# An attention and feed-forward block on one core: last pairs of a slot issued ahead of the block's copy, key differences ahead of the parts, reciprocal deviations in steps

## The chip, the cores and the metric

The kernel runs on one core of a Trainium2 chip. The metric is the device time of one execution in microseconds; the median over several executions is given. The core's engines work from queues of their own and meet only at semaphores: TensorE (PE in the profile, with its weight loads as PEld), VectorE (DVE), ScalarE (ACT), GpSimd (POOL), and SyncE (SP), which here issues most transfers.

## The reference

One transformer block in float32: layer normalisation, attention of 32 heads with 20 columns each over 2048 tokens of width 640, the input added; then a second normalisation, a gated feed-forward part of width 1728, and the sum again.

```python
def _A_ref(x, wqkv, wo):          # B, S, D = 1, 2048, 640; H = 32; Dh = 20
    qkv = (x @ wqkv).reshape(B, S, 3, H, Dh).transpose(2, 0, 3, 1, 4)
    q, k, v = qkv[0], qkv[1], qkv[2]
    scores = jnp.einsum("bhqd,bhkd->bhqk", q, k) * (Dh ** -0.5)
    p = _softmax(scores, axis=-1)
    o = jnp.einsum("bhqk,bhkd->bhqd", p, v)
    return o.transpose(0, 2, 1, 3).reshape(B, S, D) @ wo
def _B_ref(x, w_gate, w_up, w_down):
    return (_silu(x @ w_gate) * (x @ w_up)) @ w_down
h = x + _A_ref(_layernorm(x), A_wqkv, A_wo)
h2 = h + _B_ref(_layernorm(h), B_w_gate, B_w_up, B_w_down)
```

## The kernel before

The program has three stages: the projections to queries, keys and values; attention; and the output projection with the feed-forward part. The order of the work is written out by hand, and each engine runs its instructions in the order in which the program issues them. To get float32 precision out of faster matmuls, an operand is kept in two parts, `hi` and `lo`; `split` (L84) makes them, `hi` as a copy on ACT (L85), `lo` as a difference on DVE or POOL (L86).

**Projections.** The tokens come in four chunks `c` of 512. Chunk `c` has ten blocks of 128 columns (even `m` are keys, odd `m` queries; `query_key`, L429, fifteen matmuls) and eight value pieces (`value`, L500, fifteen matmuls of 320 columns). Each is a slot, numbered 18·c + j. Chunk 0 runs its blocks first, then its values; chunks 1 and 2 run five key blocks (j 0 to 4), five query blocks (j 5 to 9), eight values; chunk 3 runs keys, values, queries. In the last slots of a chunk, at j = 12 to 16 in chunk 0 and 11 to 15 in chunks 1 and 2, `flip` (L405) transposes the next chunk's normalised input: TensorE into a `ps_one` buffer, then on ACT a copy (L281) and `hi` (L85), `lo` on POOL.

The results of a block go through `keep` (L462): from slot 8 on ACT copies the block out of its buffer (L481); the parts are made in the next slot, when `finish_keep` or the next `keep` calls what was put off; then the stores are issued on ACT's own queue (L426), each block's in the slot after it. Before slot 8 the parts are made straight from the buffer, and for keys the difference of the block's two halves after them (copy L475 on ACT, subtraction L476 on DVE). A value is copied from its buffer by ACT (L517, the ev copy).

**Maxima in the projections.** The softmax needs the maximum of each query's scores over 512 keys. A part of these maxima, 288 pairs of head pairs, is computed between the projections' matmuls. `max_pair` (L170) takes two matmuls and a DVE reduction over 512 columns (L180). `max_halves` (L184) uses max(a, b) = b + relu(a − b) with the key differences: two matmuls (L188), a relu on ACT (L193), and two fused operations on DVE (L195). The operands of `max_halves` are loaded back from where the blocks were stored, as items in four `raw` tiles (`load_items`, `stack`, on SP, L148); `ready` says when an item may be used: two slots after its load was issued. Two lists hold the pairs, `urgent` (unit 0 with `max_pair`) and `early` (`max_halves`), and `visit(n)` (L358) issues up to n pairs from them that are ready. A `query_key` of chunks 1 to 3 visits once in its middle, after nine matmuls (three pairs), and the main loop visits after every slot, three pairs after a block and two after a value; a value visits in its middle too (two pairs).

**Buffers.** PSUM holds three `ps_wide` tiles of two banks (pairs; blocks of the first slots) and two `ps_one` tiles of one bank (later blocks, values, transpositions), each kind used in turn: the next user of a buffer waits until the last reader is done.

**Attention.** 32 units (a group of four heads by a chunk of queries) of sixteen steps. A step's order is in `ORDER`: scores (L950) with their exponentials on ACT (L956), the remaining maxima one at a time (matmul L204, DVE L210), and `weigh` (L960), eight matmuls with the values. In the last units `projection` runs beside it, one entry of the list `extra` a step: the output projection (L688), the sums and statistics on DVE, the reciprocal standard deviations (`moments`, fourteen small DVE operations of L95 by a first guess and three refinements, `rstd_steps`, L88), the application to the first token tile, and transpositions (L716).

Of the kernel before, what the change touches and what calls it, by code (L numbers as in the profile page):

```python
# [44 lines left out]
def tile_block(ctx: ExitStack, tc: tile.TileContext, x, wqkv, wo, wg, wu, wd, out):  # L45
# [30 lines left out]
    def ps_one():  # L76
        return psum.tile([P, CH], F32, name="ps_one", tag="ps_one", bufs=2)
# [190 lines left out]
    with tc.tile_pool(name="pa", bufs=2) as pa:  # L268
# [43 lines left out]
        def staged_keys(g, c, kc, k, q):  # L312
            def one(t, pair):
                max_halves(mxs[g * NC + c], items[q][3], items[k][3], pair, t, kc)
                for n in (k, q):
                    users[n] -= 1
                load_items()

            def ready():
                return all(items[n][3] is not None and slot[0] >= items[n][4] + 2 for n in (k, q))  # L320

            pairs = [(t, pair) for t in moved(g * NC + c, kc) for pair in range(2)]
            for n in (k, q):
                users[n] += len(pairs)
            return [(ready, lambda a=a: one(*a)) for a in pairs]
# [24 lines left out]

        urgent = [a for kc in range(NC) for a in in_unit(0, kc, 18 * kc + 7)]
        early = [a for g in range(1, NG) for a in staged(g, (0, 0))]
        early += staged(1, (0, 1)) + staged(2, (0, 1))
        early += [a for g in range(3) for a in staged(g, (1, 1), (1, 0))]
# [74 lines left out]
        def query_key(c, m):  # L429

            z_hi, z_lo = zs[c]
            ps = ps_wide()[:, 0, :] if slot[0] < 7 else ps_one()
            for n, (a, w) in enumerate(((z_hi, w_hi), (z_lo, w_hi), (z_hi, w_lo))):
                for k in range(ND):
                    nc.tensor.matmul(  # L435
                        ps, w[:, k, m * P : (m + 1) * P], a[:, k, :],
                        start=(n == 0 and k == 0), stop=(n == 2 and k == ND - 1),
                    )
                    if n == 1 and k == 3 and c:
                        visit(3)  # L440
            keep(c, m, ps)
# [22 lines left out]
        def keep(c, m, ps):  # L464
# [7 lines left out]
            if slot[0] < 8:  # L472
                split(ps, hi[:, :CH], lo[:, :CH], nc.vector)
                if which:
                    nc.scalar.activation(over, ps[:, half:], AF.Copy)  # L475
                    nc.vector.tensor_tensor(  # L476
                        out=over, in0=ps[:, :half], in1=over, op=ALU.subtract
                    )
                    halved.append(lambda: split(over, hi[:, CH:], lo[:, CH:], nc.gpsimd))
            else:  # L480
# [20 lines left out]
        def value(c, t, half):  # L501
# [5 lines left out]
            for a, w in ((z_hi, w_hi), (z_hi, w_lo), (z_lo, w_hi)):  # L507
                for k in range(ND):
# [5 lines left out]
                    if n == 9 and slot[0] > 9:  # L514
                        visit(2)
            dst = ev[:, half * 4 : half * 4 + 4, : G * VW].rearrange("p g (h w) -> p g h w", h=G)
            nc.scalar.activation(  # L517
# [39 lines left out]
        for c in range(NC):  # L557
# [7 lines left out]
            for j, (kind, *which) in enumerate(work):  # L565
# [11 lines left out]
                if which:  # L577
# [4 lines left out]
                    else:  # L582
                        (query_key if kind == "block" else value)(c, *which)
                visit(2 if kind == "value" else 3)
                finish_keep()
# [70 lines left out]
    def projection(c, ps_of):  # L656
# [41 lines left out]

        def moments():
            rs.append(rstd_of(pc, mv[:, :, 1], TPC, "c"))  # L700

# [25 lines left out]
        def first(t, half):  # L727
# [8 lines left out]
            [lambda t=t, half=half: first(t, half) for t in range(TPC) for half in range(2)],  # L736
            [moments, lambda: apply(0)],
            [lambda t=t: flip(t) for t in range(TPC)],
# [287 lines left out]
    for u in range(NU):  # L1026
        g, c = divmod(u, NC)
        if g == NG - 1 and c >= 2:
            _, first, ln, flips, _ = ahead
            extra = [*first, ln[0], lambda: None, ln[1], lambda: None, *flips]  # L1030
        for kt in range(NT):
# [626 lines left out]
```

## Time and profile before

| | us |
|---|---|
| median of three executions | 2107.35 (2106.49 to 2111.93) |
| the profiled execution's own time | 2110.45 |
| its span, first to last instruction | 2108.7 |
| projections | 0 to 389.5 |
| attention | 389.5 to 1536.5 |
| output projection and feed-forward | 1536.5 to 2108.7 |

The mean granted clock of TensorE over the span is 0.995 of full speed. The page's slices show its busy share and its clock, in tenths, in 40 slices of 52.7 us:

```
PE   7999999999999999999999999999999999999998
PEclk9999999999999999999999999999999999999999
```

The projections are the first seven or so of these slices. A timeline row has the start and the duration of a group of equal instructions, the engine, the line, the output and input tiles by name, and in brackets the idle time before it with the instruction that ended it. A window's row has the busy times of the engines inside two borders.

### The profile page before, as it was taken

The numbers are of one execution on the slowest core, as the hardware profiler recorded it, in microseconds if no ns is written. First come the engines' busy times: TensorE is split into PE (matmuls) and PEld (weight loads), VectorE is DVE, ScalarE is ACT, GpSimd is POOL, SyncE is SP. The second block draws the span as 40 slices with busy tenths as digits, with TensorE's granted clock in tenths as the row PEclk, the third lists the DMA queues.
The fourth block names the chain that finished last, engine by engine and source line by source line (L and its number), as shares of the span: only waits on it lengthen the run. The fifth ranks groups of instructions, "written<-read, shape, count | busy, mean of one in ns | idle before, by whom it ended". The sixth has DMA issues, their size and how long they took to land.

```text
span 2108.7 us, 37142 instructions
## 1 busy us (share of the span) xinstructions
PE 2066.6 (98%) x12636; PEld 1207.3 (57%) x12636; DVE 1659.5 (79%) x3631; ACT 1445.4 (69%) x2835; POOL 691.2 (33%) x949
## 2 busy tenths in 40 slices
PE   7999999999999999999999999999999999999998
PEld 5656566433333433334333433335578888888888
DVE  6767867788888888888888988886368766666677
ACT  3647575899999999999999999996743222212221
POOL 2231110233443424353420001001135434653555
PEclk9999999999999999999999999999999999999999
DMA  8565544335263443543631213131137755884642
GB/s 257 174 205 179 164 140 127 87 116 153 88 183 103 148 140 118 156 139 133 188 111 56 52 32 94 34 115 61 35 121 266 263 169 188 298 301 159 196 152 94
DMA packets 197285, 305.38 MB, mean 145 GB/s; under 512 B 47440, under 2 KB 82256, under 8 KB 196072
## 3 DMA queue, kind: packets, MB, share of 16 engines
q1 hardware_dynamic: 183512, 274.15, 41.2%
q10 hardware_dynamic: 13584, 28.85, 4.6%
q8 instruction: 102, 1.67, 0.4%
q14 instruction: 87, 0.71, 0.1%
HBM read 203.82 MB, written 98.30 MB: 143 GB/s over the span
## 4 chain that ended last, share of the span: by engine, by line
PE 87%; DVE 6%; DMA 3%; issue 2%; ACT 1%; ACTq 1%; POOL 0%; SPq 0%; DVEq 0%; POOLq 0%
PE acc L960 24%; PE ps_one L950 15%; PE ps_a L1121 15%; PE ps_max L204 12%; PE ps_b L1215 8%; PE ps_one L509 3%; PE ps_wide L188 3%; PE ps_one L435 3%; DVE over L195 2%; PE ps_max L688 2%; DVE mx L180 2%; PE ps_b L688 1%; DMA halves<-j_d 1%; ACTq L426 1%; ACT over L193 0%
## 5 line engine op out<-in xcount | busy, mean ns | idle before, releaser
L956 ACT ACTIVATE probs<-ps_one 128x512 f32<-128x512 f32 x2048 | 1056.9, 616 | 66.1 <-PE ps_one L950 41.3
L210 DVE TENSOR_REDUCE mx<-ps_max 128x1 f32<-128x512 f32 x1472 | 925.6, 683 | 109.3 <-PE ps_one L950 77.6
L950 PE MATMUL ps_one<-q_stk,k_stk 62*128 62x512 f32 x2048 | 586.4, 451 | 2.6 <-DVE m L86 1.7
L960 PE MATMUL acc<-probs,v_stk 128*32 128x512 f32 x4096 | 547.2, 607 | 0.0
L950 PEld LDWEIGHTS ps_one<-q_stk,k_stk 62*128 62x128 f32 x2048 | 251.6, 184 | 432.9 <-ACT probs L956 397.1
L204 PE MATMUL ps_max<-k_stk,q_stk 60*128 60x512 f32 x1472 | 381.7, 425 | 1.4 <-DVE mx L210 1.3
L204 PEld LDWEIGHTS ps_max<-k_stk,q_stk 60*128 60x128 f32 x1472 | 271.9, 186 | 26.6 <-DVE mx L210 2.7
L195 DVE CUSTOM_DVE_ANT_0 over<-ps_wide,over 128x256 f32<-128x256 f32 x512 | 184.7, 420 | 82.9 <-ACT over L193 82.8
L1336 DVE TENSOR_TENSOR tmp<-ps_a,tmp 128x512 f32<-128x512 f32 x208 | 141.2, 689 | 119.9 <-PE ps_a L1121 94.1
L193 ACT ACTIVATE over<-ps_wide 128x512 f32<-128x512 f32 x256 | 138.6, 597 | 76.9 <-PE ps_wide L188 32.2
L1215 PE MATMUL ps_b<-halves,yp 128*128 128x320 f32 x1032 | 179.3, 308 | 2.0 <-DMA halves<-j_d 1.2
L960 PEld LDWEIGHTS acc<-probs,v_stk 128*32 128x32 f32 x4096 | 80.7, 108 | 175.3 <-issue 166.7
L1215 PEld LDWEIGHTS ps_b<-halves,yp 128*128 128x128 f32 x1032 | 165.1, 188 | 18.6 <-POOL yp L86 1.5
L995 POOL TENSOR_TENSOR o<-o,rb 128x512 f32<-128x512 f32 x31 | 39.9, 1286 | 411.2 <-DMA q_stk<-q_d 178.8
L1121 PE MATMUL ps_a<-t,units 128*128 128x512 f32 x624 | 162.6, 396 | 0.0
L1121 PE MATMUL ps_a<-z,units 128*128 128x512 f32 x516 | 133.9, 394 | 0.0
L1121 PEld LDWEIGHTS ps_a<-t,units 128*128 128x128 f32 x624 | 112.6, 188 | 18.8 <-ACT tmp L1349 0.2
L86 POOL TENSOR_TENSOR yp<-y,yp 128x256 fp32r<-128x256 f32 x96 | 60.2, 627 | 188.3 <-ACT yp L85 188.3
L188 PE MATMUL ps_wide<-raw 60*128 60x512 f32 x512 | 107.6, 468 | 12.3 <-DVE mx L195 7.1
L1220 DVE TENSOR_TENSOR h<-ps_b,h 128x320 f32<-128x320 f32 x248 | 109.9, 480 | 6.9 <-PE ps_b L1215 5.4
L1121 PEld LDWEIGHTS ps_a<-z,units 128*128 128x128 f32 x516 | 93.1, 187 | 15.9
L85 ACT ACTIVATE yp<-tmp 128x512 fp32r<-128x512 f32 x40 | 25.3, 632 | 103.1 <-POOL tmp L1208 103.1
(189 smaller groups left out, 2195.5 us busy)
## 6 DMA issues: line engine op xcount, KB each, us to landing
units<-w_d SPq DMA_DIRECT2D x186, 256.0 KB
w_d<-stage SPq DMA_DIRECT2D x106, 256.0 KB
halves<-j_d SPq DMA_DIRECT2D x70, 320.0 KB
j_d<-stage SPq DMA_DIRECT2D x42, 320.0 KB
k_stk<-k_d SPq DMA_DIRECT2D x64, 160.0 KB
q_stk<-q_d SPq DMA_DIRECT2D x64, 160.0 KB
raw<-k_d SPq DMA_DIRECT2D x54, 160.0 KB
rb<-r_d SPq DMA_DIRECT2D x32, 256.0 KB
```

What stands on the lines that cost most here:

```text
L188: nc.tensor.matmul(ps[:, b, :], q[rows, pair, t * P : (t + 1) * P], k[rows, pair, :], start=True, stop=True,)
L193: nc.scalar.activation(over, ps[:, :, CH // 2 :], AF.Relu)
L195: nc.vector.tensor_tensor_reduce(over[:, b], ps[:, b, : CH // 2], over[:, b], 1.0, LOWEST, ALU.add, ALU.max, mx[:, b, pair, t, kc : kc + 1],)
L204: nc.tensor.matmul(ps, queries[u][rows, pair, t * P : (t + 1) * P], keys[u // NC][rows, pair, kc * CH : (kc + 1) * CH], start=True, stop=True,
L210: nc.vector.tensor_reduce(mxs[u][:, b, pair, t, kc : kc + 1], ps, axis=AX.X, op=ALU.max)
L950: nc.tensor.matmul(ps, keys[u // NC][rows, p, kt * P : (kt + 1) * P], queries[u][rows, p, :], start=True, stop=True,)
L956: nc.scalar.activation(probs[p][:, b, :], ps, AF.Exp, scale=scale)
L960: nc.tensor.matmul(acc[32 * j : 32 * j + 32, :], values[u // NC][:, kt, j * VW : j * VW + 32], probs[j // 2][:, j % 2, :], start=(kt == 0) ...
L1121: nc.tensor.matmul(ps.rearrange("p (t n) -> p t n", t=TPC), w[k][:, i], z[k][:, :, j], start=(first and m == 0), stop=(last and m == len(n ...
L1215: nc.tensor.matmul(ps, a, b, start=(n == 0), stop=(n == len(pairs) - 1))
L1220: nc.vector.tensor_tensor(out=h, in0=ps, in1=h, op=ALU.add)
L1336: add = lambda out, ps, x: nc.vector.tensor_tensor(out=out, in0=ps, in1=x, op=ALU.add)
```

## The change

It has five edits in the projections and one in attention.

1. `ready`: in slots below 24 an item may be used three slots after its load was issued, later two as before.
2. The eight pairs of unit 0 against the second chunk of keys leave `urgent` (where they were `max_pair`) and join `early` as `max_halves`; two more items are loaded for them.
3. The block of slot 6 uses a `ps_one` buffer; before, it used half a `ps_wide`.
4. Pairs ahead of the copies: in chunks 1 to 3 a block's last `visit(3)` is issued before `keep`, so before its copy; in the middle it visits two pairs where m is a multiple of four, three otherwise. A value's last `visit(2)` is issued before the ev copy. The main loop's own visit is left for the blocks of chunk 0.
5. In the slots below 8 the key difference (L475, L476) is issued ahead of the parts (L85, L86).
6. `moments` runs in three attention steps, five, five and four of its operations, and the application follows in the third. Before, all fourteen ran in one step, and the application two steps later. The list `extra` keeps its length.

```diff
             def ready():
-                return all(items[n][3] is not None and slot[0] >= items[n][4] + 2 for n in (k, q))
+                return all(items[n][3] is not None and slot[0] >= items[n][4] + 2 + (slot[0] < 24) for n in (k, q))
...
-        urgent = [a for kc in range(NC) for a in in_unit(0, kc, 18 * kc + 7)]
+        urgent = [a for kc in (0, 2, 3) for a in in_unit(0, kc, 18 * kc + 7)]
         early = [a for g in range(1, NG) for a in staged(g, (0, 0))]
-        early += staged(1, (0, 1)) + staged(2, (0, 1))
+        early += [a for g in range(3) for a in staged(g, (0, 1))]
...
-            ps = ps_wide()[:, 0, :] if slot[0] < 7 else ps_one()
+            ps = ps_wide()[:, 0, :] if slot[0] < 6 else ps_one()
...
                     if n == 1 and k == 3 and c:
-                        visit(3)
+                        visit(2 if m % 4 == 0 else 3)
+            if c:
+                visit(3)
             keep(c, m, ps)
...
             if slot[0] < 8:
-                split(ps, hi[:, :CH], lo[:, :CH], nc.vector)
                 if which:
                     nc.scalar.activation(over, ps[:, half:], AF.Copy)
                     nc.vector.tensor_tensor(
                         out=over, in0=ps[:, :half], in1=over, op=ALU.subtract
                     )
+                split(ps, hi[:, :CH], lo[:, :CH], nc.vector)
+                if which:
                     halved.append(lambda: split(over, hi[:, CH:], lo[:, CH:], nc.gpsimd))
...
                     if n == 9 and slot[0] > 9:
                         visit(2)
+            visit(2)
             dst = ev[:, half * 4 : half * 4 + 4, : G * VW].rearrange("p g (h w) -> p g h w", h=G)
...
-                visit(2 if kind == "value" else 3)
+                if c == 0 and kind != "value":
+                    visit(3)
                 finish_keep()
...
-        def moments():
-            rs.append(rstd_of(pc, mv[:, :, 1], TPC, "c"))
+        chain = []
+
+        def moments(i):
+            if not rs:
+                r, steps = rstd_steps(pc, mv[:, :, 1], TPC, "c")
+                rs.append(r)
+                chain.extend(steps)
+            for f in chain[5 * i : 5 * i + 5]:
+                f()
...
-            [moments, lambda: apply(0)],
+            [lambda: moments(0), lambda: moments(1), lambda: (moments(2), apply(0))],
...
-            extra = [*first, ln[0], lambda: None, ln[1], lambda: None, *flips]
+            extra = [*first, *ln, lambda: None, *flips]
```

## The prediction

> **What bounds the kernel now.** I read the head of the page, the table of windows, then the timeline at the places that the diff touches. First the span, the engines' busy times and the engines' shares of the chain that ended last.
>
> ```profile
> span 2108.7 us, 37142 instructions
> PE 2066.6 (98%) x12636; PEld 1207.3 (57%) x12636; DVE 1659.5 (79%) x3631; ACT 1445.4 (69%) x2835; POOL 691.2 (33%) x949
> PE 87%; DVE 6%; DMA 3%; issue 2%; ACT 1%; ACTq 1%; POOL 0%; SPq 0%; DVEq 0%; POOLq 0%
> ```
>
> TensorE is busy for 98%, and the diff takes no matmul away: the maxima of all 288 pairs stay, so only TensorE's idle and slowly clocked time can shrink. Next the windows: borders and length, busy time and instructions of PE, PEld, DVE, ACT, POOL, then granted clock, DMA share, GB/s. The first two are projections and attention; the third holds the blocks of chunk 1, the fourth its slot 21; the last three lie in the attention step that the diff's last part touches.
>
> ```profile
> 0.00:389.51 389.51, 361.29 (x1773) 247.42 (x1773) 281.22 (x1210) 228.02 (x420) 79.29 (x66) 0.98 0.58 175
> 389.51:1536.50 1146.99, 1143.64 (x7890) 469.86 (x7890) 976.97 (x1653) 1080.66 (x2132) 314.40 (x472) 1.00 0.35 105
> 97.71:163.85 66.14, 60.15 (x257) 39.49 (x256) 45.68 (x184) 33.03 (x59) 19.32 (x15) 0.95 0.71 205
> 114.86:126.93 12.07, 8.64 (x28) 5.26 (x26) 4.14 (x21) 3.62 (x7) 3.27 (x3) 0.72 0.73 220
> 1464.00:1468.00 4.00, 2.71 (x17) 0.90 (x15) 3.55 (x18) 3.37 (x7) 0.00 (x0) 1.00 0.35 139
> 1468.00:1472.00 4.00, 3.88 (x15) 1.34 (x17) 3.50 (x6) 1.08 (x2) 0.00 (x0) 0.57 0.00 0
> 1476.00:1480.00 4.00, 4.00 (x24) 1.41 (x21) 0.27 (x2) 2.84 (x7) 0.00 (x0) 0.67 0.00 0
> ```
>
> The projections leave TensorE idle for 389.51 − 361.29 = 28.2 us, attention for 3.4; those and the two slow clocks (0.72, 0.57 to 0.67) are all there is to win. So I price each slot by TensorE's instructions and stalls.
>
> **Blocks of chunks 1 to 3.** Timeline rows: start, duration, engine, instruction; in brackets the idle time before and what ended it. A slot begins with the first L435.
>
> ```profile
> 110.17 1.45 PE L435 MATMUL ps_one<-z_hi,w_hi 128*128 128x512 f32 x5
> 114.86 1.30 PE L435 MATMUL ps_one<-z_hi,w_hi 128*128 128x512 f32 x5
> 131.36 1.30 PE L435 MATMUL ps_one<-z_hi,w_hi 128*128 128x512 f32 x5
> 134.77 1.29 PE L435 MATMUL ps_one<-z_hi,w_hi 128*128 128x512 f32 x5
> 200.43 1.43 PE L435 MATMUL ps_one<-z_hi,w_hi 128*128 128x512 f32 x5
> 205.16 0.89 PE L188 MATMUL ps_wide<-raw 60*128 60x512 f32 x4
> 206.24 0.49 PE L188 MATMUL ps_wide<-raw 60*128 60x512 f32 x2 [0.19 <-DVE mx L195]
> 206.67 0.50 PE L435 MATMUL ps_one<-z_hi,w_hi 128*128 128x512 f32 x1
> ```
>
> A slot without pairs takes 134.77 − 131.36 = 3.41, with three in its middle 114.86 − 110.17 = 4.69, with 3 + 3 it takes 206.67 − 200.43 = 6.24. The last pair of the 3 + 3 doesn't start when two pairs' 0.89 are over (206.05) but at 206.24, for DVE. Hence estimates: 2 + 3 pairs 5.55 (a middle pair and that wait less), 3 + 2 5.45, 3 + 1 5.15.
>
> Where m is a multiple of four the change makes 3 + 3 into 2 + 3; the later readiness and the eight pairs of unit 0 turned from `max_pair` to `max_halves` shift the rest. Counting by the code's own rules I get, for slots 18 to 28, 5, 3, 5, 3, 5, 3, 6, 6, 4, 6, 2 pairs, against 6, 6, 3, 6, 2, 0, 0, 6, 6, 6, 4. Their prices sum to 3 × 5.55 + 3 × 4.69 + 3 × 6.24 + 5.15 + 3.5 = 58.1, against the window's 66.14: −8.0. What the old slot 21 lost is in that:
>
> ```profile
> 118.45 0.46 PE L188 MATMUL ps_wide<-raw 60*128 60x512 f32 x1 [1.39 <-DMA raw<-q_d]
> 120.95 1.61 PE L188 MATMUL ps_wide<-raw 60*128 60x512 f32 x5 [2.04 <-DMA raw<-q_d]
> 115.97 4.89 DMA raw<-q_d
> ```
>
> It waited 1.39 + 2.04 us for a load that lands at 115.97 + 4.89 = 120.86 (the third row is from the chain of waits), and ran at 0.72. The load is issued in slot 19 as before; with the extra slot of readiness its first user is slot 22. Measured from slot 18's start (97.71) it lands at 23.15; the new slot 22 comes to its middle pairs at 5.55 + 4.69 + 5.55 + 4.69 + 2.3 = 22.8, where 2.3 are the nine matmuls ahead of them. So half a microsecond of wait is left; I charge 0.7: **−7.3**. Bounds: −8.7 (the load comes earlier by what slot 18 saves) to −2.2 (the wait and the slow clock come back whole).
>
> In chunk 2, slots 36, 38, 40 change from 6.24 to 5.55 (−2.1), 39 and 41 lose 0.4 each, later ones 0.4; the first of the next slot's pairs after a 2 + 3 finds ACT later, +0.4: **−2.9**, bounds 0 and −3.5. In chunk 3, slots 54, 56, 58 give −2.1, 57 and 68 with a pair fewer −1.6, one more in 55 +0.2. The last slot, 71, gets 3 + 1 pairs that ran earlier. They stand ahead of attention's first scores:
>
> ```profile
> 388.87 0.60 ACT L481 ACTIVATE e<-ps_one 128x512 f32<-128x512 f32 x1 [1.52 <-PE ps_one L435]
> 389.51 0.73 PE L950 MATMUL ps_one<-q_stk,k_stk 62*128 62x512 f32 x3 [0.69 <-ACT e L481]
> ```
>
> The scores wait for the block's copy, 0.04 after its end; with a pair and its relu ahead of that copy and three pairs in the middle I charge 2.1. Sum of chunk 3 **−1.4**, bounds −2.5 and +1. In all of these the moved `visit` also issues a block's relus ahead of its copy on ACT; the copy, its hi copy and the stores run in the next slot, beside TensorE's first ten matmuls there. What happens if that cover is short is a rival below.
>
> **Value slots.** Here the same reordering meets another buffer rule. One value slot that is followed by a transposition:
>
> ```profile
> 172.78 0.97 PE L509 MATMUL ps_one<-w_hi,z_hi 128*128 128x320 f32 x5
> 176.01 0.85 PE L188 MATMUL ps_wide<-raw 60*128 60x512 f32 x4
> 176.12 0.44 ACT L517 ACTIVATE ev<-ps_one 128x320 f32<-128x320 f32 x1 [0.22 <-PE ps_one L509]
> 176.58 1.08 ACT L193 ACTIVATE over<-ps_wide 128x512 f32<-128x512 f32 x2
> 176.79 0.66 PE L405 MATMUL ps_one<-ident,xt 128*128 128x128 f32 x4
> 177.20 0.98 PE L509 MATMUL ps_one<-w_hi,z_hi 128*128 128x320 f32 x5
> 177.55 0.60 ACT L281 ACTIVATE e<-ps_one 128x512 f32<-128x512 f32 x1
> ```
>
> `ps_one` has two buffers: the value takes one, the transposition the other, so the next value takes the first again, which the ev copy (L517) must have read. Before, that copy ends at 176.12 + 0.44 = 176.56, and the next value starts at 177.20 without a wait. After, two relus go first; L281 shows when ACT is through with the like (177.55, after the ev copy and two relus whose second needs a pair that ends at 176.86). The copy then runs from about 177.52 to 177.96, the next value starts at 178.00: +0.80. There are 15 such slots (12 to 16, 29 to 33, 47 to 51); some have slack, one has a pair fewer, so I take **+10.8** for 12.0, bounds 0 (the copy finds a gap) and +15 (the hi copies behind it are late too).
>
> **First block copies.** In slots up to 7 the key difference (L475, L476) goes ahead of the parts (L85, L86).
>
> ```profile
> 47.97 0.38 ACT L475 ACTIVATE e<-ps_wide 128x256 f32<-128x256 f32 x1 [1.01 <-DVE e L86]
> 48.87 0.80 PE L176 MATMUL ps_wide<-k_stk,q_stk 60*128 60x512 f32 x2 [2.70 <-DVE e L476]
> ```
>
> ACT's L475 starts only when DVE's L86 is done with the same buffer, and the pair's matmuls wait for L476. All four operations read one buffer and ACT and DVE alternate on it, so another order leaves the chain as long; slot 6's block in `ps_one` lets a pair wait for an older buffer. I take **−0.4**, bounds 0 and −1.4. [...]
>
> **Reciprocal deviations.** In attention the fourteen small DVE operations of L95 run in one go, the last at 1467.23:
>
> ```profile
> 1467.23 0.16 DVE L95 TENSOR_TENSOR r_c<-r_c,t_c 128x4 f32<-128x4 f32 x1
> 1468.05 1.39 PE L204 MATMUL ps_max<-k_stk,q_stk 60*128 60x512 f32 x2 [1.34 <-DVE mx L210]
> 1465.21 1.07 PE L960 MATMUL acc<-probs,v_stk 128*32 128x512 f32 x8
> 1469.96 1.93 PE L960 MATMUL acc<-probs,v_stk 128*32 128x512 f32 x8
> 1474.91 1.70 PE L960 MATMUL acc<-probs,v_stk 128*32 128x512 f32 x8
> 1477.69 1.50 PE L960 MATMUL acc<-probs,v_stk 128*32 128x512 f32 x8
> ```
>
> The maxima queue up behind them, TensorE waits 1.34 for their buffer, and the clock row behind shows 0.57, later 0.67. Half steps take 4.75 (1469.96 − 1465.21) and 4.95, the next 2.78. Cut in three, five of 0.16 us and their gaps a time, DVE keeps up; with 2.7 for each of the two I get −4.3. Bounds −5 and −1.3 (the wait alone). The same fourteen in the next unit meet no maxima any more and cost nothing either way.
>
> **Sum** against the profiled run's own 2110.45 (span 2108.7 and 1.75 around it): −0.4 + 10.8 − 7.3 − 2.9 − 1.4 − 4.3 = −5.5, so 2105.0. That run lies 3.1 above the median of the three, 2107.35; the difference put on the median is **2101.9**.
>
> **Rivals.**
> *The value slots' wait doesn't arise.* For it: TensorE stands 0.64 behind the ev copy now, and relus may fit there. Against: the two-buffer sequence. Without the 10.8 the time is 2091.1. Chance 0.18.
> *Slower: copies behind relus, stores behind copies.* After a 3 + 3 block ACT runs three relus, the block's copy, its hi copy, and issues stores:
>
> ```profile
> 211.62 1.36 ACTq L426 DMA_DIRECT2D k_d<-e  x3
> 377.45 2.15 ACTq L426 DMA_DIRECT2D q_d<-e  x3
> ```
>
> Issuing takes 1.36 to 2.15. If the next slot's middle pairs, 2.3 after its start, wait for ACT behind that train, each slot pays what the train exceeds the cover by; eleven slots of 3 + 3 at 0.8 make +8.8: 2110.7. It decides from 0.5 a slot (11 × 0.5 = 5.5). For it: the 2.15. Against: the same train lay in the same place relative to the middle relus, less one copy, and those slots took 6.24. Chance 0.14.
> *Load wait and slow clock come back in slot 22:* +5.1, 2107.0. For: the margin is half a microsecond short. Against: 0.5 is far from 3.4. Chance 0.10.
> *The slow stretch in attention stays:* only 1.3 comes back, 2104.9. For: a gap of 1.34 is short beside the 4 us rows, so its part in the clock isn't shown. Against: the low clock begins right behind it. Chance 0.08. [...]
>
> **How the numbers follow.** The forecast has 0.50, with its own range 2098 to 2106 from the bounds of chunk 1 and the value slots. About 0.3%, 6.3 us, is what a measurement of this kernel can tell from no change: under 2101.0 is faster, over 2113.7 slower. Faster: 0.18 and half of the forecast, with some of the last two's lower ends, 0.45. Slower: the upper half of the slower rival, and the slower rival or the load wait on top of a value slot's +15, 0.12. Same 0.43. The range runs from the first rival, 2091, to the slower one, 2111.
>
> **What would show it.** Right: value slots of 5.2 us where they took 4.43, with TensorE waiting for L517's copy at the next value; no wait for `raw` over 1 us in slots 18 to 28, and 58 to 59 us for them; even half steps of 2.6 to 2.8 at the L95 operations with the clock at 1. Wrong: value slots unchanged (then 2091), waits of TensorE for L193 or L195 in the middle of blocks (then the slower rival), or a clock below 1 in the new slot 22 or the attention step.

## The result, and the profile after

The changed kernel takes 2118.26 us (median of five executions, 2117.53 to 2121.2), the kernel before 2107.35 (2106.49 to 2112.13). The ratio is 1.0047 with a 95% interval of 1.0031 to 1.0062: slower by 6.5 to 13 us. Forecast were 2101.9 and, at most, 2111. The profiled execution took 2117.61 against 2110.45 before, so the traces explain 7.2 us.

The head of the changed kernel's page, then its table of windows (borders and length, busy time of PE, PEld, DVE, ACT, POOL, clock, DMA share, GB/s): the projections, slots 18 to 28, slots 22, 25, and 29 with 30, and two stretches of the attention step with the divided moments.

```profile
span 2115.8 us, 37211 instructions
PE 2068.1 (98%) x12636; PEld 1207.7 (57%) x12636; DVE 1658.8 (78%) x3655; ACT 1445.7 (68%) x2843; POOL 692.8 (33%) x949
```

```profile
0.00:402.90 402.90, 365.62 (x1774) 247.86 (x1775) 280.21 (x1234) 228.57 (x428) 79.11 (x66) 0.97 0.57 173
99.56:167.01 67.45, 62.11 (x264) 40.43 (x262) 44.82 (x223) 38.68 (x71) 18.88 (x15) 0.92 0.67 210
119.94:129.91 9.97, 7.34 (x27) 4.54 (x25) 4.39 (x23) 3.48 (x7) 3.74 (x3) 0.83 0.76 242
140.69:151.70 11.01, 8.65 (x29) 5.03 (x28) 5.95 (x29) 4.34 (x9) 1.28 (x1) 0.76 0.59 197
167.01:183.81 16.80, 12.46 (x56) 8.63 (x54) 7.99 (x39) 6.82 (x15) 1.79 (x2) 0.80 0.44 125
1478.00:1482.00 4.00, 4.00 (x28) 1.31 (x25) 3.73 (x15) 3.60 (x8) 0.00 (x0) 1.00 0.22 88
1482.00:1486.00 4.00, 3.95 (x26) 1.56 (x18) 3.79 (x10) 3.40 (x8) 0.00 (x0) 1.00 0.00 0
```

The projections end at 402.90 where they ended at 389.51: +13.4. Attention gives 4.2 back in the unit with the moments, where the clock is now 1.00 throughout. The rest is 2.1 shorter; that lies behind attention, where nothing was edited, so none of the six edits accounts for it. Where the 13.4 lie shows in the view of TensorE's waits in the projections (what waited and for whom, us in total, times, longest). Before:

```profile
PE ps_wide L188 <- DVE mx L195: 7.1, 24, 0.9
PE ps_wide L188 <- DMA raw<-q_d: 3.4, 2, 2.0
```

After:

```profile
PE ps_one L512 <- ACT ev L521: 8.7, 15, 0.9
PE ps_wide L188 <- DMA raw<-q_d: 7.4, 4, 3.6
PE ps_wide L188 <- DVE mx L195: 3.6, 12, 1.1
PE ps_one L962 <- DVE mx L195: 1.6, 1, 1.6
```

Half of DVE's waits went, as the edit of the pairs should bring. A wait for the ev copy came in 15 slots, and the waits for `raw` doubled. In slots, each from its first matmul to the next slot's, in us:

| slots | before | after | difference | forecast |
|---|---|---|---|---|
| start of slot 10 | 61.25 | 59.86 | −1.4 | −0.4 |
| values 12–16 | 22.54 | 25.89 | +3.4 | +3.6 |
| 18–28 | 66.14 | 67.45 | +1.3 | −7.3 |
| values 29, 30 | 8.93 | 16.80 | +7.9 | +1.4 |
| values 31–33, 47–51 | 35.59 | 42.17 | +6.6 | +5.8 |
| 36–45 | 64.42 | 61.28 | −3.1 | −2.9 |
| 54 to the first scores | 94.93 | 94.05 | −0.9 | −1.4 |

(The forecast for the values is the 10.8 shared over 15 slots.) Two rows are off: 18 to 28 by 8.6, and 29, 30 by 6.5. The rest came out near its price. In short, the value slots cost what was forecast, and late loads in slots 22, 25 and 29, with the slow clock behind them (0.83, 0.76 and 0.80 in the windows above), cost some 15 us that were not.

### The profile page after: what moved, and what is told of

Its sections match the earlier page's. It is cut to its first block, busy times and chain, and to the rows that moved or that the text cites. A ratio compares the mean times of both kernels' runs of the same rounds, so it can differ in the third digit from the quotient of the medians.

```text
span 2115.8 us, 37211 instructions
## 1 busy us (share of the span) xinstructions
PE 2068.1 (98%) x12636; PEld 1207.7 (57%) x12636; DVE 1658.8 (78%) x3655; ACT 1445.7 (68%) x2843; POOL 692.8 (33%) x949
## 4 chain that ended last, share of the span: by engine, by line
PE 79%; DVE 1%; DMA 1%; ACT 1%; POOL 0%; issue 0%; SPq 0%; ACTq 0%; DVEq 0%; POOLq 0%
PE acc L972 24%; PE ps_one L962 15%; PE ps_a L1133 15%; PE ps_max L204 12%; PE ps_b L1227 8%; PE ps_max L693 2%; PE ps_b L693 2%; PE ps_one L435 1%; DMA halves<-j_d 1%; PE ps_wide L188 0%; DVE over L195 0%; PE ps_max L728 0%; PE ps_one L512 0%; POOL h L1265 0%; ACT o L982 0%
## 5 line engine op out<-in xcount | busy, mean ns | idle before, releaser
L195 DVE CUSTOM_DVE_ANT_0 over<-ps_wide,over 128x256 f32<-128x256 f32 x528 | 191.2, 421 | 104.6 <-ACT over L193 104.4
L86 POOL TENSOR_TENSOR yp<-y,yp 128x256 fp32r<-128x256 f32 x96 | 60.4, 629 | 188.0 <-ACT yp L85 180.0
L85 ACT ACTIVATE yp<-tmp 128x512 fp32r<-128x512 f32 x40 | 25.3, 632 | 103.3 <-POOL tmp L1220 103.3
```

The lines of the kernel that those rows point to most:

```text
L195: nc.vector.tensor_tensor_reduce(over[:, b], ps[:, b, : CH // 2], over[:, b], 1.0, LOWEST, ALU.add, ALU.max, mx[:, b, pair, t, kc : kc + 1],)
```

## The experiments

Every run was timed beside the kernel before. The "reordered base" is the changed kernel with a value's last pairs behind the ev copy again (the first run).

| run | median us | ratio to before (95%) |
|---|---|---|
| e1_value_pairs_after_copy | 2103.95 | 0.9976 (0.9964 to 0.9987) |
| e2_unit0_pairs_unstaged | 2114.52 | 1.0023 (1.0011 to 1.0034) |
| e3_ready_two_slots | 2119.86 | 1.0047 (1.0032 to 1.0061) |
| e4_moments_only | 2103.51 | 0.9974 (0.9965 to 0.9984) |
| e5_gaps_closed | 2103.46 | 0.9969 (0.9955 to 0.9982) |
| e6_input_load_early | 2103.11 | 0.9970 (0.9960 to 0.9981) |
| e7_one_pair_each_side | 2111.09 | 1.0010 (0.9998 to 1.0022) |
| e8_staged_unit0_only | 2110.07 | 1.0001 (0.9991 to 1.0011) |
| e9_steps_and_chunk2 | 2101.06 | 0.9962 (0.9949 to 0.9976) |
| e10_queries_load_later | 2097.81 | 0.9950 (0.9932 to 0.9968) |
| e11_both_loads_later | 2094.35 | 0.9933 (0.9915 to 0.9952) |
| e12_no_input_loads | 2097.46 | 0.9948 (0.9930 to 0.9966) |
| e13_inputs_ahead_of_items | 2093.89 | 0.9933 (0.9912 to 0.9953) |
| e14_no_pairs_in_slot_71 | 2094.59 | 0.9938 (0.9916 to 0.9960) |

### The value's last pairs

```diff
-            visit(2)
             dst = ev[:, half * 4 : half * 4 + 4, : G * VW].rearrange("p g (h w) -> p g h w", h=G)
...
-                if c == 0 and kind != "value":
-                    visit(3)
+                if c == 0 or kind == "value":
+                    visit(2 if kind == "value" else 3)
```

> The changed kernel with one edit undone: a value's last two pairs are issued behind the ev copy again. Ring theory: the next value waits for the ev copy of the value before the transposition (same buffer of two), 0.83 us in each of about 14 slots between 12 and 51; without the edit those slots go back to 4.4 to 4.6 us and the time falls by 11 to 12 us, to about 2106.5. Rival: the slots are long because ACT as a whole is full (relus, copies, hi copies) and its order does not matter; then they stay near 5.25 us and the time near 2118. The three waits for raw loads in slots 22, 25 and 29 stay in both.

The time fell by 14.3 us, the projections end at 386.32. The end of slot 12 on the timeline, first in the changed kernel (start, duration, engine, instruction, wait; TensorE and ACT):

```profile
72.88 0.90 PE L188 MATMUL ps_wide<-raw 60*128 60x512 f32 x4
73.47 0.60 ACT L193 ACTIVATE over<-ps_wide 128x512 f32<-128x512 f32 x1 [0.65 <-ACT over L193]
73.71 0.66 PE L405 MATMUL ps_one<-ident,xt 128*128 128x128 f32 x4
...
73.96 0.59 ACT L193 ACTIVATE over<-ps_wide 128x512 f32<-128x512 f32 x1
74.44 0.44 ACT L521 ACTIVATE ev<-ps_one 128x320 f32<-128x320 f32 x1
...
74.94 0.85 PE L512 MATMUL ps_one<-w_hi,z_hi 128*128 128x320 f32 x4 [0.57 <-ACT ev L521]
```

then in the reordered base:

```profile
75.56 0.92 PE L188 MATMUL ps_wide<-raw 60*128 60x512 f32 x4
75.66 0.44 ACT L520 ACTIVATE ev<-ps_one 128x320 f32<-128x320 f32 x1 [0.16 <-PE ps_one L512]
...
76.40 0.66 PE L405 MATMUL ps_one<-ident,xt 128*128 128x128 f32 x4
76.81 0.39 PE L512 MATMUL ps_one<-w_hi,z_hi 128*128 128x320 f32 x1
```

In the first, two relus run before the ev copy, which ends at 74.88; the next value starts 0.06 later. In the second the copy is done at 76.10, before the transposition starts, and the value follows that without a wait. All slots 47 to 51 went from 5.26–5.31 back to 4.43–4.50. Slot 25 lost its wait too (6.32), slots 22 and 29 kept theirs.

Half the dose, one pair on each side:

```diff
-            visit(2)
+            visit(1)
             dst = ev[:, half * 4 : half * 4 + 4, : G * VW].rearrange("p g (h w) -> p g h w", h=G)
...
-                if c == 0 and kind != "value":
-                    visit(3)
+                if c == 0 or kind == "value":
+                    visit(1 if kind == "value" else 3)
```

> The changed kernel with one of a value's last two pairs ahead of the ev copy and one behind it. Ring theory: the copy then waits for one relu (about 0.54 us) instead of two, ends near 0.4 us after the last pair's matmuls, and the next value waits about 0.3 us: value slots followed by a transposition take 4.65 to 4.85 us, halfway between 4.43 and 5.27. Rival: any relu ahead of the copy makes the value wait for the copies behind it; then 5.2 as before. The time falls by some 6 to 8 us against the changed kernel.

Slots 47 to 51 take 4.77 to 4.83: 0.34 above 4.43, where two relus cost 0.83. Each relu ahead of the copy cost the next value 0.34 to 0.42 us here.

### The pairs of unit 0

```diff
-        urgent = [a for kc in (0, 2, 3) for a in in_unit(0, kc, 18 * kc + 7)]
+        urgent = [a for kc in range(NC) for a in in_unit(0, kc, 18 * kc + 7)]
         early = [a for g in range(1, NG) for a in staged(g, (0, 0))]
-        early += [a for g in range(3) for a in staged(g, (0, 1))]
+        early += staged(1, (0, 1)) + staged(2, (0, 1))
```

> The changed kernel with one edit undone: unit 0's eight pairs against the second chunk of keys are max_pair again, from the keys already in place, and no loads are made for them. Load theory: the eight pairs needed no load and covered slots 25 and 26; turned into staged pairs they add two loads and let TensorE reach the items of slots 25 and 29 one to two slots earlier than before, when their loads have not landed. Undone, the waits of 2.4 us in slot 25 and 3.6 us in slot 29 and the slow clock behind them go, about 10 us, while max_pair's reductions cost slots 25 and 26 about 1 us: time near 2109. Rival: the loads are late because the blocks' copies, and so the stores that the loads read, stand behind relus on ACT; then waits over 2 us stay in slots 25 and 29 and the time stays near 2118. The wait in slot 22 stays in both.

> The kernel before with only unit 0's eight pairs staged (two more items, no other edit). Load theory: this edit alone makes TensorE reach the new items early: waits for raw over 1 us in slots 24 or 25 and in slot 29, with slow stretches behind, 5 to 10 us more than before. Rival: the waits there need the stores to be late as well, as they are with the pairs ahead of the copies; then no wait over 1 us shows after slot 22 and the time is within 2 us of before.

These are TensorE's waits of the changed kernel in slot 25 (first two rows) and slot 29:

```profile
144.85 0.47 PE L188 MATMUL ps_wide<-raw 60*128 60x512 f32 x1 [1.13 <-ACT over L193]
146.54 0.79 PE L188 MATMUL ps_wide<-raw 60*128 60x512 f32 x1 [1.23 <-DMA raw<-q_d]
172.54 0.70 PE L188 MATMUL ps_wide<-raw 60*128 60x512 f32 x3 [3.56 <-DMA raw<-q_d]
```

Undone in the changed kernel, slot 25 falls from 11.01 to 6.66, slot 29 from 9.95 to 5.34, slot 30 from 6.85 to 5.27, as the load theory has it; slot 22 keeps its wait (10.96). (In slot 25 the view puts 1.13 us of the old waits down to a relu and only 1.23 to a load.) The time is 2114.5, not 2109: with that order eight pairs were left to slot 71, which took 10.05 instead of 6.89, and attention ran at half clock for 6.8 us from 398.0, by the trace's record of the granted clock. The run e8 makes the edit, the reverse of the lines above, alone in the kernel before. It leaves the time level, 2110.07; slots 24, 25 and 29 take 8.86, 8.31 and 8.09 against 3.40, 6.66 and 4.50. In that profile the projections end at 395.03, 5.5 us later than before; why the medians show nothing of it stays open. Neither expectation there was quite right: the long slots come, but only slot 29's waits are a load's or a store's; in slot 24 ACT stood behind two stores (3.39 us of issuing) and its relus came late, and slot 25 ran at half clock for 4.6 of its 8.3 us (granted clock 0.72 over the slot).

Slot 29 is the plainest marker over the profiles (the four runs that move a load out of its way follow below):

| | slot 29, us |
|---|---|
| unit 0's pairs staged: after, e1, e3, e6, e7, e8, e12 | 9.95, 9.00, 10.75, 9.50, 10.39, 8.09, 8.48 |
| not staged: before, e2, e4, e5, e9 | 4.50, 5.34, 4.49, 5.33, 4.50 |

### The readiness rule

```diff
-                return all(items[n][3] is not None and slot[0] >= items[n][4] + 2 + (slot[0] < 24) for n in (k, q))
+                return all(items[n][3] is not None and slot[0] >= items[n][4] + 2 for n in (k, q))
```

> The changed kernel with one edit undone: below slot 24 an item may again be used two slots after its load. Theory: the load of group 7's queries is late whatever the slot that first asks for it, since it stands behind the input loads and a store on the SP queue; without the extra slot, slot 21 asks for it and TensorE waits there by about one slot longer (slot 21 near 12 us, slot 22 near 4.5), while slots 18 to 21 hold more pairs; the time stays within 2 us of 2118. Rival: the extra slot only thins the early slots and so causes the crowd of pairs in slots 24 to 29; then the waits in slots 25 and 29 shrink by over 1 us each and the time falls by 3 or more.

Slot 21 took 9.68 and slot 22 4.42, the time stayed. The extra slot moves the wait and doesn't take it away. Over the profiles, slot 21 with the old rule takes 12.08, 7.20, 9.68, 8.44 and 10.07 (before, e4, e3, e8, e9) against 6.24 without a wait. So 12.08, from which the prediction took its gain, was the worst of five samples; the projections of before and of e4 are the same code, and give 12.08 and 7.20. With the new rule and the old input loads slot 22 takes 8.8 to 11.0 (after, e1, e2, e6, e7, e10, e11) against a price of 5.55.

The other way to get clear of the wait was to ask later still, together with the edits of e1 and e2:

```diff
-                return all(items[n][3] is not None and slot[0] >= items[n][4] + 2 + (slot[0] < 24) for n in (k, q))
+                return all(items[n][3] is not None and slot[0] >= items[n][4] + 2 + 2 * (20 < slot[0] < 24) for n in (k, q))
...
-                        visit(2 if m % 4 == 0 else 3)
+                        visit(2 if m % 4 == 0 and c < 3 else 3)
```

> The changed kernel with the value's last pairs behind the ev copy again, unit 0's eight pairs unstaged again, and the readiness rule replaced: in slots 21 to 23 an item waits four slots, elsewhere two; two pairs in the middle where m is a multiple of four only in chunks 1 and 2. Load theory: slots 21 and 22 then hold no pairs (3.4 us each), group 7's items are first used in slot 23, and no wait for raw over 1 us is left in slots 18 to 30; slots 18 to 28 together 58 to 60 us against 62.4 in the moments-only kernel's profile and 66.1 before; chunk 2 and 3 gain some 5 us as in the kernel with the value's pairs behind the copy. Time 2094 to 2097. Rival: loads are late by contention that follows the pairs wherever they go; then waits over 2 us appear in slots 23 to 29 and the time is 2100 or more.

The waits for loads went (0.53 us in one place), but slot 23, where six pairs now stand, took 9.75. On its timeline TensorE waits for DVE, and DVE had nothing, because ACT was issuing stores and making parts:

```profile
125.43 2.19 ACTq L426 DMA_DIRECT2D k_d<-e  x3
127.67 0.84 ACT L85 ACTIVATE e<-e 128x768 fp32r<-128x768 f32 x1 [3.70 <-DMA k_d<-e]
128.42 1.55 ACT L193 ACTIVATE over<-ps_wide 128x512 f32<-128x512 f32 x3
...
129.95 0.50 PE L188 MATMUL ps_wide<-raw 60*128 60x512 f32 x2 [2.97 <-DVE mx L195]
```

The three relus start at 128.42, some 3 us after their matmuls. With slots 21 and 22 empty of pairs, key blocks follow each other every 3.4 us, and the work behind a block (difference and parts on POOL and ACT, then the stores) falls behind. So the gap closed in one place opens in another: neither the load theory nor its rival. In this slot ACT's stores and parts are the bound.

### The order on the SP queue

In these traces SP issues its transfers one after the other, and where one waits, those behind it do too: in the changed kernel the input loads are issued from 104.56 to 111.29, the key half of slot 22's items from 111.38 to 117.75, the query half from 117.80. The first try to move chunk 2's input loads forward set their issue at the end of slot 17:

```diff
-                    if c > 0:
+                    if c > 1:
                         load_x(c + 1)
...
+                if (c, j) == (0, 17):
+                    load_x(2)
```

> The kernel with the value's pairs behind the ev copy (time 2103.95), and chunk 2's input loads issued at the end of slot 17, one slot ahead. Theory: in slot 22 the load of group 7's queries is late because its issue stands on the SP queue behind the input loads, and those behind a value store whose semaphore they share; issued early they are gone by then, and slot 22 falls from 10.5 to about 5.5 us. Rival: the load is late because the key and query blocks of the same chunk are stored at the same time and the transfers share bandwidth; then slot 22 stays above 8 us.

This told nothing: slot 17's raw loads are issued in that slot as well and stayed ahead, and the input loads started at 102.76 where they had started at 103.17. Slot 22 took 9.70. Leaving the loads out did tell:

```diff
             for t in range(c * TPC, (c + 1) * TPC):
+                if c == 2:
+                    xs[t] = xs[t - TPC]
+                    continue
                 xs[t] = pa.tile([P, D], F32, name="xt", tag="xt", bufs=4)
```

> The kernel with the value's pairs behind the ev copy, without the loads of chunk 2's input: chunk 2 is computed from the tiles of chunk 1. This leaves out four transfers of 320 KB on the SP queue and no other work. Theory: group 7's queries are late for slot 22 because of these transfers and the store they wait for; without them slot 22 falls from 10.5 to 5.5 us. Rival: the load is late because the stores of the same chunk's keys fill the transfer engines, or because ACT, which issues them in order, is behind; then slot 22 stays above 8.

Slot 22 fell to 6.37, with no wait for a load. Its middle pairs on the timeline:

```profile
116.91 1.07 PE L438 MATMUL ps_one<-z_lo,w_hi 128*128 128x512 f32 x4
117.91 0.98 PE L188 MATMUL ps_wide<-raw 60*128 60x512 f32 x4
118.81 0.50 PE L438 MATMUL ps_one<-z_lo,w_hi 128*128 128x512 f32 x1
```

In the changed kernel the same place reads:

```profile
123.65 0.47 PE L188 MATMUL ps_wide<-raw 60*128 60x512 f32 x1 [1.49 <-DMA raw<-q_d]
125.27 0.70 PE L188 MATMUL ps_wide<-raw 60*128 60x512 f32 x3 [1.15 <-DMA raw<-q_d]
```

The run takes away the loads' traffic together with their place in the queue, so it doesn't tell the two apart. SP's own rows show where the time goes. From the input loads to slot 22's items, first in the kernel before, then in the changed one, with two rows of the latter's view of SP's waits (95 to 205 us; total, times, longest):

```profile
100.62 4.04 SPq L277 DMA_DIRECT2D xt<-in_A_x  x4
109.72 3.44 SPq L148 DMA_DIRECT2D raw<-k_d  x4
113.21 3.10 SPq L148 DMA_DIRECT2D raw<-q_d  x4
```

```profile
104.56 6.73 SPq L277 DMA_DIRECT2D xt<-in_A_x  x4
111.38 6.37 SPq L148 DMA_DIRECT2D raw<-k_d  x4
117.80 3.35 SPq L148 DMA_DIRECT2D raw<-q_d  x4
```

```profile
SPq L148 <- DMA k_d<-e: 7.5, 4, 3.3
SPq L277 <- DMA v_d<-ev: 5.0, 1, 5.0
```

Measured from slot 18's start, the key half's first issue is no later than before (11.8 for 12.0). But its four issues take 6.37 us instead of 3.44, and the query half follows 2.7 later (18.2 for 15.5). Among the four, SP stands 3.3 us for the landing of a key block's store, which ACT issued; among the input loads it stands 5.0 for a value's store. So here stores held up the queue as well as loads. The kernel before has such a wait too, 5.0 for a value's store, but behind its input loads. What earlier stores would be worth no run tests.

Slot 29 stayed long in the run without the input loads (8.48); its cause is another transfer. On the SP queue of the changed kernel, the query half of slot 29's items stands behind a load that only attention needs:

```profile
157.73 1.51 SPq L148 DMA_DIRECT2D raw<-k_d  x4
159.28 4.84 SPq L148 DMA_DIRECT2D q_stk<-q_d  x4
164.16 5.08 SPq L148 DMA_DIRECT2D raw<-q_d  x4
```

Moved to slot 31, on the reordered base:

```diff
-                if j == (4 if c == 0 else 8) and c < 3:
+                if j == (4, 13, 8, -1)[c]:
                     load_queries(c)
```

> The kernel with the value's pairs behind the ev copy, and the load of unit 1's queries, first needed in attention, issued in slot 31 instead of slot 26. Queue theory: the last item for slot 29 is late because its load stands behind that load on the SP queue; slot 29 falls from 9.0 to 9.5 to about 5 us, slots 22 to 25 as before. Rival: the item is late because its tile comes free, or its block is stored, too late for any order; then slot 29 stays above 8.

```profile
150.10 1.51 SPq L148 DMA_DIRECT2D raw<-k_d  x4
151.72 5.02 SPq L148 DMA_DIRECT2D raw<-q_d  x4
```

The query half follows the key half at once, and slot 29's pairs run without a wait:

```profile
160.76 0.73 PE L188 MATMUL ps_wide<-raw 60*128 60x512 f32 x4
```

The slot falls from 9.00 to 4.54, and the time by 6 us to 2097.81. Then the keys of chunk 1 for attention as well, which no pair of the projections reads once unit 0's are staged:

```diff
-                if j == (4 if c == 0 else 3):
+                if j == (4, 13, 3, 3)[c]:
                     load_keys(0, slice(c * CH, (c + 1) * CH))
```

> As the run with the queries' load in slot 31, and the load of group 0's keys of chunk 1 (640 KB), which no pair of the projections needs any more, issued in slot 31 instead of slot 21. Queue theory: the items for slots 24 and 25 are issued about 4 us earlier; slots 24 and 25 together fall to 12.3 us (13.2 to 13.5 in the two kernels with the value's pairs behind the copy), slot 29 near 5; slot 22, whose items are issued ahead of that load, stays near 10. Rival, as for the queries' load.

Slots 24 and 25 take 12.43, slot 29 4.63, slot 22 still 9.83, the time 2094.35: faster than both kernels. (The intervals of this run and the one before it overlap; that the second move helps rests on slots 24 and 25, 14.12 before it.) Its window from slot 18 to slot 28:

```profile
96.17:157.81 61.64, 58.56 (x264) 38.43 (x262) 43.45 (x223) 37.58 (x69) 18.20 (x14) 0.97 0.72 221
```

That is 5.8 us less than in the changed kernel for the same pairs, and 1.9 less than in the reordered base (63.52). Last, the input loads at the end of slot 16, ahead of slot 17's raw loads (with the condition at slot 18 changed as in e6), and a version of that without pairs in slot 71:

```diff
+                if (c, j) == (0, 16):
+                    load_x(2)
```

> The kernel with both attention loads later, and chunk 2's input loads issued at the end of slot 16, ahead of slot 17's raw loads on the SP queue; same transfers, other place. Theory (place): the input loads are through before group 7's items are asked for, slot 22 falls from 9.8 to 5.5 to 6.4 us as it did without those loads, slot 29 stays near 4.6: 2090 to 2092. Rival (traffic): the same bytes still compete with the key stores, and slot 22 stays above 8.

```diff
-                        visit(2)
+                        visit(3 if slot[0] in (52, 53, 65, 66) else 2)
```

> As the run with the input loads ahead, and a third middle pair in the value slots 52, 53, 65 and 66, so that slot 71 has no pairs left. Theory: the first scores wait only for the block's copy, slot 71 takes 4.4 instead of 6.9 us and no slow stretch follows it; the four pairs cost about 0.65 us each where they go; the time is level with the run before it or 2 us lower. Rival: pairs cost the same wherever they stand and the slow stretch comes anyway; then no change, with a clock below 1 at attention's start.

Slot 22 took 6.87 in the first and 8.84 in the second, whose code is the same up to there, against 9.83 with the loads in slot 18 (e11) and 6.37 without them (e12). Both are below the 9.83, as place would have it, and above the 6.37; whether that remainder is traffic or scatter, one profile each doesn't tell. Slot 71 took 4.38 without pairs instead of 6.92, but slots 36 to 71 together 189.8 instead of 189.1, so the pairs cost as much where they went. The slow clock at attention's start lasted 6.8 us in one and 3.4 in the other, so it came without pairs in slot 71 too. Both times are level with 2094.35.

### The moments, and the pairs of chunk 2

> The kernel before with only the last edit: the fourteen small operations in three attention steps. Theory: the single burst made TensorE wait 1.34 us and then run at half clock for two stretches; in steps both go, and the time falls by 4.1 us, to 2103.2, with the granted clock at 1 throughout the unit. Rival: the low clock comes from something else in that unit; then only 1.3 us come back, 2106.0, and rows with a clock near 0.6 remain behind the operations.

The edit is number 6 of the change, made in the kernel before. The time fell by 5.4 us (0.9965 to 0.9984 are 3.4 to 7.4). Window behind the operations, first of this run, then of the run e8, which has the burst:

```profile
1465.00:1469.00 4.00, 3.94 (x20) 1.50 (x20) 3.65 (x14) 3.39 (x8) 0.00 (x0) 1.00 0.00 0
```

```profile
1469.00:1473.00 4.00, 2.98 (x21) 1.15 (x17) 3.55 (x17) 3.54 (x7) 0.00 (x0) 1.00 0.34 136
```

In the profile the unit is 4.2 us shorter than before, and so it is, to a tenth, in the changed kernel and in all other profiles with the steps but one: in e10 a slow stretch of 3.4 us came in that unit all the same, and it is 2.9 shorter. The burst without a slow clock, as in e8, costs 2.4 less than before's; so of the 4.2 the waits are 1.8 and the clock 2.4. Of the two profiles with the burst one has the slow clock there, of the fourteen with the steps one. So the burst alone doesn't decide it; but the 3.4 to 7.4 of the whole time are more than the waits' 1.8.

> The kernel before with the moments in steps, and the reordering of pairs kept only where it paid: the last pairs ahead of the copy in the blocks of chunks 2 and 3, two pairs in the middle where m is a multiple of four in chunk 2 only, and a third middle pair in the value slots 52, 53, 59, 60, 65, 66, which have no transposition behind them, so that slot 71 has none. Theory: slots 36 to 71 fall by 4 to 5 us against the moments-only kernel, attention starts without the 1.65 us wait and without a slow stretch: 2098 to 2100. Rival: the gain in chunk 2 is only pairs pushed to later slots; then slots 36 to 71 sum to within 2 us of the moments-only kernel's 196.75 and the time stays near 2103.

The edit, in the kernel before with the moments in steps:

```diff
-                        visit(3)
+                        visit(2 if m % 4 == 0 and c == 2 else 3)
+            if c > 1:
+                visit(3)
             keep(c, m, ps)
...
-                        visit(2)
+                        visit(3 if slot[0] in (52, 53, 59, 60, 65, 66) else 2)
...
-                visit(2 if kind == "value" else 3)
+                if c < 2 or kind == "value":
+                    visit(2 if kind == "value" else 3)
```

Slots 36 to 71 sum to 193.0 against 196.75, a gain of 3.7 for the same pairs. The kernel before, whose code there is that of the moments-only kernel, has 195.3, so the gain is 2.3 to 3.7: less than the theory's 4 to 5, and somewhat more than pairs pushed about. The time is 2101.06, 2.5 below the moments-only kernel; the two intervals overlap. Attention starts without a slow stretch, as expected.

## Why the prediction failed

**The step that failed.** Two terms of the sum were wrong, both about loads. The first is the load wait of slot 22: "The load is issued in slot 19 as before; with the extra slot of readiness its first user is slot 22. Measured from slot 18's start (97.71) it lands at 23.15". The landing was taken over from one profile as if it were fixed to the slot's start. In the changed kernel the query half landed near 25.7 after slot 18's start (125.27 − 99.56), and TensorE waited 1.49 + 1.15 us and then ran slowly (granted clock 0.83 over the slot): slot 22 took 9.97 instead of 5.55. The load's landing hung on SP's queue. There it stands behind four input loads of 320 KB, which started 5.0 us after slot 18's start (104.56 − 99.56) instead of 2.9 (100.62 − 97.71), and behind waits for stores of 5.0 and 3.3 us. Without the input loads the wait went (6.37); with them earlier in the queue slot 22 took 6.87 and 8.84. How much of it is the loads' place, their traffic and the stores isn't shared out. The rival "load wait and slow clock come back in slot 22" had that right, with +5.1 for a measured 4.4, and was given 0.10.

**What the sum lacked** is larger: the new loads stood in it at nothing. The change turns eight pairs that need no load into pairs that need two. The prediction counted them as pairs per slot and looked at one load only; it never asked, for the items of slots 25 and 29, what stands ahead of them on SP's queue. Slots 25, 29 and 30 cost 4.8, 4.7 and 1.6 more than their prices of 6.24, 5.26 and 5.26. That staging them is the cause in slot 29 is shown by undoing it; that the mechanism there is the queue is shown by the queries' load moved (e10), which takes the wait away with the pairs still staged. Slot 25's wait went with the staging undone, but also in the reordered base (6.32), so there a shift of the blocks by some microseconds is enough; why the wait came there stays open.

**The −8.0 itself** was taken from one execution. The kernel before and e4 have the same code in slots 18 to 28, and their profiles give 66.14 and 62.43. Against the second the same prices make −4.3.

**What held.** The value slots: the two-buffer rule, the 0.80 a slot (0.83 measured) and the sum near 11 to 12; the rival in which that wait doesn't arise falls. Chunk 2 (−3.1 for −2.9) held. Chunk 3's −0.9 for −1.4 includes 1.2 in slot 64, a value slot outside the fifteen, which wasn't foreseen and is gone with the value's pairs put back (4.12 in e1); attention's start, priced at 2.1, took 6.89 − 4.42 = 2.5:

```profile
400.75 0.50 PE L188 MATMUL ps_wide<-raw 60*128 60x512 f32 x2
402.90 0.50 PE L962 MATMUL ps_one<-q_stk,k_stk 62*128 62x512 f32 x2 [1.65 <-DVE mx L195]
```

It is the last pair's reduction, not the copy alone, that the first scores wait for. The early blocks' −1.4 is one sample: slots 7 to 9 sum to 20.97 on average in the twelve profiles with the edits and 21.54 in the four without, −0.6 for −0.4, but single profiles spread from 19.70 to 22.83, so that isn't clear of scatter. The −0.4 was the author's estimate, and no run shows the term by itself. What the traces show of it is that ACT's and DVE's reads of one buffer follow each other in both orders: before, L475 waits 1.01 us for DVE's L86, and in slot 6 of the changed kernel ACT's hi copy waits 0.95 for DVE's subtraction and starts 0.03 behind its end (46.62):

```profile
46.20 0.42 DVE L477 TENSOR_TENSOR e<-ps_one,e 128x256 f32<-128x256 f32 x1
46.65 0.60 ACT L85 ACTIVATE e<-ps_one 128x512 fp32r<-128x512 f32 x1 [0.95 <-DVE e L477]
```

The moments' total held to a tenth, partly by luck. Of the two half steps that were to fall to 2.7 the first did (4.75 to 2.66), the second fell from 4.95 only to 4.07, although the clock was at 1; the three behind it made up for that (2.78, 2.85 and 3.15 to 1.95, 2.54 and 3.02). The rival with only 1.3 falls, since the run with the steps alone gave 3.4 to 7.4.

**The slower rival** named another mechanism, relus held up behind copies and stores on ACT. In chunks 2 and 3 it didn't show: blocks of 2 + 3 pairs took 5.5 and of 3 + 3 6.2, as priced. It did show where slots without pairs let the blocks run ahead (2.97 us in e5, and slot 24 in e8), and the 1.13 us put down to a relu in slot 25 of the changed kernel is of its kind.

By the profiled executions the forecast was −5.5 and the result +7.2: the miss of 12.7 is 8.6 in slots 18 to 28 and 6.5 in slots 29 and 30, less 2.4 in other places.

## What to carry to other kernels

Asking one slot later didn't remove the wait for a transfer here (slot 21 took 9.68 under the old rule in e3, slot 22 took 9.97 under the new one); follow the queue that issues it, and list all that stands ahead. When work that needs no load is turned into work that does, price the new loads at the queue, together with the loads of other stages that could go later: here moving two such loads, needed only in attention, took 9.6 us off the median, of which the profiles show 6.2 in slots 18 to 71. With two buffers and an alternating user, look at what is put ahead of a buffer's last reader: here one relu there cost the next-but-one owner 0.34 us, two cost 0.83.

## What the runs showed of the hardware

The same code gave slot 21 at 12.08 and at 7.20, so a stall read from one profile is a sample. In the trace's record of the granted clock the slow stretches that begin and end within the span are at 0.50: in the kernel before 6.8 us from 48.43 and from 120.11 and 3.4 from 1468.37 and from 1475.20, in the changed kernel 3.4 from 47.45 and from 125.95 and 6.8 from 146.44 and from 173.74. In the kernel before, the wait of 1.34 us in attention is followed by the two stretches of 3.4 (no other wait of TensorE from 1440 to 1482 is over 0.21 us); in e8 the same wait of 1.34 in the same unit is followed by none. In e10 a stretch of 3.4 came in that unit (from 1462.92) although the profile has no wait of TensorE over 0.04 us in it. (Four score matmuls just ahead, each released by ACT, take 1.97 us and may hide short waits; but the half step that holds them is as long, 4.08, in profiles without the stretch.) So a wait of 1.34 us need not bring the slow clock, and it can come where the profile names no wait; what decides it no run here shows.
